# Gated linear attention and an expert layer in one kernel: units of two chunks, position pairs, weights by the quarter

## The chip, the cores and the metric

One core of one Trainium2 chip. The metric is the device time of one execution in microseconds (us). Five engines work side by side: PE (matmul; PEld is its weight load), VectorE (DVE), ScalarE (ACT), GpSimd (POOL) and SyncE (SP, here a queue of DMA issues). The kernel fixes the order of instructions on each engine itself.

## The reference, cut to what matters

```
f = sigmoid(f_logit)                                  # q, k, v, f_logit: (4, 8, 768, 48), float32
for t in range(768):                                  # for each of 4 batches and 8 heads
    state = f[t, :, None] * state + outer(k[t], v[t]) # 48 x 48
    y[t] = q[t] @ state
x = y, heads side by side                             # (3072, 384)
h = x @ w_in                                          # (3072, 2048)
out = (0.5 * h * (1 + erf(h / sqrt(2)))) @ w_out      # (3072, 384), float32
```

## The kernel before

The 768 positions of each batch are cut into six chunks of 128, 24 chunks in all, with a position on each partition and the eight heads side by side. A chunk is loaded by four DMAs of SP, f_logit, k, q and v (L299 and L302), each 192 KB in runs of 48 floats, 192 bytes. ScalarE makes exp and ln of f_logit (L319, L323); PE sums the logs down the chunk with a triangular matrix (L335) and makes the chunk's total decay (L337); ScalarE takes exp of both signs (rg L341, gt L344, gl L347); VectorE multiplies k and q by them (L350, L354); GpSimd casts v (L358). In `attn(n)` PE turns k and q so that the head dimension lies on partitions (L378), VectorE copies them out (kq, L383), PE makes the scores of four pairs of heads in eight matmuls (L392), VectorE masks them (L396). PE makes the chunk's own state (L406), VectorE and GpSimd carry the state from chunk to chunk (L417, L421, L423, L428), PE adds the carried state's part and the chunk's own part of y (L442, L448). VectorE copies y out (L454), PE turns it (L462), VectorE writes it as the columns of x that belong to the chunk (L464).

The second half works on groups of chunks (`SIZES`: four groups of one, then ten of two). F1 multiplies x by `w_in` in blocks that fill one PSUM bank (L485), ScalarE puts each block through gelu (L490), F2 multiplies by `w_out` (L500), ScalarE copies the result out (L504) and SP stores it (L506). Both weights are bf16 tiles in SBUF, one for each matrix (`win`, `wout`, L201 and L202), each loaded in four quarters by GpSimd's DMA queue, which also casts them from float32 (L305, L309).

The order comes from a planner (`Plan.run`, L90): each operation has an engine, an estimated duration, what it reads and writes, and buffers; the operation with the earliest possible start is placed next, a tie is broken by `prio`. An ACT operation that needs the other table (exp and ln in one, gelu in the other) has its start put 2 x 1.28 us later for the comparison. The planner's order is then issued as it stands, engine by engine. `LOADS` fixes the order of the loads: chunks 0 to 3, the four quarters of `win` (i0 to i3), chunk 4, two quarters of `wout` (o0, o1), chunk 5, o2, o3, then the rest. Where the next load is on another queue than the one before it, it waits for the landing of an earlier load on that other queue: the third before it for a load of GpSimd, the second before it for a load of SP. SP also issues the stores, in the planner's order.

PSUM has eight banks: four for F1 and F2 (`s_fh`), two for the scores (`s_ap`), two for all else (`s_m`).

Of the kernel before, what the change touches and what calls it, by code (L numbers as in the profile page):

```python
# [16 lines left out]
TABLE = 1.28  # L17

# [37 lines left out]
class Op:  # L56
    __slots__ = ("eng", "dur", "fn", "bufs", "prio", "deps", "table", "start", "end", "vis", "seq", "name",
                 "left", "outs", "inst", "gate")


class Plan:
# [6 lines left out]
    def add(self, eng, dur, fn, rd=(), wr=(), bufs=(), prio=0.0, deps=(), table=None, name=""):  # L68
# [3 lines left out]
        o.gate = ()  # L72
        o.seq = len(self.ops)
        d = list(deps)
# [15 lines left out]
    def run(self):  # L90
        free = dict.fromkeys(list(LAT), 0.0)
# [9 lines left out]
        while ready:  # L101
            best = None
            for o in ready:
                t = free[o.eng]
                for d in o.deps:
                    v = d.end if d.eng == o.eng and o.eng != "DMA" else d.vis
                    t = v if v > t else t
# [12 lines left out]
                if o.table and act and o.table != act:  # L120
                    x += 2 * TABLE
# [40 lines left out]
def kernel(  # L162
# [36 lines left out]
    mask = one.tile([C, C], BF16, name="mask")  # L199
    negcol = one.tile([C, 1], BF16, name="negcol")  # L200
# [10 lines left out]
    s_gl = slots(10, [C, P2], F32, "gl")  # L211
    s_kq = slots(3, [C, 2, P2, C], BF16, "kq")
    s_am = slots(6, [C, P2, C], BF16, "am")
# [15 lines left out]
    P.add("POOL", 0.5, lambda: tri(trin, -1.0), wr=["trin"], prio=-100)  # L229
    P.add("POOL", 0.5, lambda: make_identity(nc, ident), wr=["ident"], prio=-90)  # L230
    P.add("POOL", 0.5, lambda: tri(mask, 1.0), wr=["mask"], prio=-80)
    P.add("POOL", 0.1, lambda: nc.gpsimd.memset(negcol, -1.0), wr=["negcol"], prio=-99)
# [19 lines left out]
    n = 0  # L252
    els = []
    for s in ELS:
        els.append(dict(ns=list(range(n, n + s)), fl=s_fl.new(), lf=s_lf.new()))
        for j in range(s):
            X[n + j].update(el=els[-1], j=j)
        n += s
    for n in range(NCH):
        for nm in ("kt", "qt", "vt"):  # L260
            X[n][nm] = s_in[nm].new()
# [3 lines left out]
    order = []  # L265

    def load(eng, what, issue, wr, bufs, dur, name):
# [5 lines left out]
        def fn():  # L273
            o.inst = issue()
            if i and order[i - 1][0] != eng:
                back = 3 if eng == "pool" else 2
                for j in range(i - back, -1, -1):
                    if order[j][0] != eng and order[j][1].inst is not None:
                        tc.add_manual_dep(
                            o.inst.ins, order[j][1].inst.ins.name,  # L280
                            mybir.DependencyInfo(mybir.DependencyClass.Sync, mybir.DependencyReason.DATA),
                            reason="one transfer after another")
                        break
        o.fn = fn
        return o
# [7 lines left out]
    last = None  # L293
    for what in LOADS:
        m = int(what[1:])
        if what[0] == "c":
            x = X[m]
            e = x["el"]
            load("sp", "f", lambda x=x, e=e, m=m: nc.sync.dma_start(out=e["fl"].t()[:, x["j"]], in_=src(f_logit, m)),  # L299
                 [("f", m)], [e["fl"]], 1.03, f"ldf{m}")  # L300
            for nm, a in (("kt", k), ("qt", q), ("vt", v)):
                load("sp", nm, lambda x=x, nm=nm, a=a, m=m: nc.sync.dma_start(out=x[nm].t(), in_=src(a, m)),  # L302
                     [(nm, m)], [x[nm]], 1.03, f"ld{nm}{m}")
        elif what[0] == "i":
            load("pool", what, lambda m=m: nc.gpsimd.dma_start(  # L305
                out=win[:, :, 512 * m:512 * m + 512], in_=win_src[:, :, 512 * m:512 * m + 512]),
                [f"win{m}"], [], 2.2, what)
        else:
            load("pool", what, lambda m=m: nc.gpsimd.dma_start(out=wout[:, 4 * m:4 * m + 4, :], in_=wo_src[m]),  # L309
                 [f"wout{m}"], [], 2.2, what)  # L310


    def decays(lo, hi, gate):
        made = []
        pr0 = 10 * lo
        for e in [e for e in els if lo <= e["ns"][0] < hi]:
            ns, s, fl, lf = e["ns"], len(e["ns"]), e["fl"], e["lf"]
            pr = 10 * ns[0]
            made.append(P.add("ACT", 0.04 + 0.34 * s, lambda fl=fl, s=s: nc.scalar.activation(  # L319
                fl.t()[:, 0:s], fl.t()[:, 0:s], AF.Exp, scale=-1.0),  # L320
                rd=[("f", n) for n in ns], wr=[("e", n) for n in ns], bufs=[fl], table="exp", prio=pr, deps=gate,
                name=f"E{ns[0]}"))
            P.add("ACT", 0.04 + 0.34 * s, lambda fl=fl, lf=lf, s=s: nc.scalar.activation(  # L323
                lf.t()[:, 0:s, :, 0:D], fl.t()[:, 0:s], AF.Ln, bias=1.0),
                rd=[("e", n) for n in ns] + z_lf, wr=[("lf", n) for n in ns], bufs=[fl, lf], table="exp", prio=pr,
                name=f"L{ns[0]}")
            for j, n in enumerate(ns):
                x = X[n]
# [236 lines left out]
```

## Time and profile before

| | us |
|---|---|
| median of three runs | 228.24 |
| the three runs | 226.05, 228.24, 228.71 |
| the profiled execution | 228.91 |
| its span, first to last instruction | 227.1 |
| PE busy in it | 187.8 (83%) |
| ACT busy | 126.5 (56%) |
| DVE busy | 103.8 (46%) |
| POOL busy | 49.0 (22%) |
| mean granted clock of PE | 0.985 |

Busy times are of one profiled execution. A busy PE is not PE at its peak, since a wait for weights and a lower clock count as busy too. What an engine waited for is inferred from semaphores.

### The profile page before, as it was taken

What the parts mean: (1) busy time and instruction counts of PE and PEld (TensorE: products, weight loads), DVE (VectorE), ACT (ScalarE), POOL (GpSimd) and SP (SyncE); (2) the same over time, 40 slices, a digit from 0 to 9 for tenths busy, and PEclk for the clock granted to TensorE, in tenths of its full rate; (3) what the DMA queues carried; (4) which work ended last, traced back from release to release, by engine and by line L of the source; (5) the groups of instructions that cost most, each with busy time, mean ns of one, the idle gap of its engine ahead of it and who ended that gap; (6) DMA issues with size and microseconds to landing.
All of it is one profiled execution on the core that took longest, in us unless ns stands there. A gap on an engine that the chain in (4) does not pass through costs nothing. (4 is left out here: it accounts for less than half of the span.)

```text
span 227.1 us, 4959 instructions
## 1 busy us (share of the span) xinstructions
PE 187.8 (83%) x1984; PEld 147.7 (65%) x1984; DVE 103.8 (46%) x210; ACT 126.5 (56%) x234; POOL 49.0 (22%) x99
## 2 busy tenths in 40 slices
PE   0666436199896789979969968999999999999993
PEld 0444236199564577767758657778788696878871
DVE  3788401000174374795887849779767200000000
ACT  4444022049622848597588687869297182736550
POOL 2236231302020150342226035233211000000000
PEclk9999999999999589999999999999999999999999
DMA  7998437998708994999999899981020001010101
GB/s 133 187 187 119 71 42 138 160 178 141 143 32 211 190 194 74 196 198 179 207 202 184 168 205 197 184 179 36 0 72 4 35 35 38 35 67 6 69 0 71
DMA packets 105495, 27.06 MB, mean 119 GB/s; under 512 B 100352, under 2 KB 104960, under 8 KB 105472
## 3 DMA queue, kind: packets, MB, share of 16 engines
q1 hardware_dynamic: 103296, 23.60, 55.3%
q0 software_dynamic: 2176, 3.15, 9.1%
q8 instruction: 15, 0.25, 0.5%
q14 instruction: 8, 0.07, 0.1%
HBM read 25.17 MB, written 4.72 MB: 132 GB/s over the span
## 5 line engine op out<-in xcount | busy, mean ns | idle before, releaser
L485 PE MATMUL ps<-xT,win 128*128 128x256 bf16 (+1 forms) x672 | 77.4, 275 | 13.8 <-DMA win<-in_moe_w_in_dram 13.4
L485 PEld LDWEIGHTS <-win 128*128 128x128 bf16 x672 | 67.0, 119 | 16.5 <-DMA win<-in_moe_w_in_dram 14.1
L490 ACT ACTIVATE gT<-ps 128x512 bf16<-128x512 f32 x96 | 55.1, 600 | 37.0 <-PE ps L485 34.0
L500 PE MATMUL ps<-wout,gT 128*128 128x384 bf16 x384 | 68.9, 326 | 0.0
L500 PEld LDWEIGHTS <-gT 128*128 128x128 bf16 x384 | 35.7, 98 | 20.1
L396 DVE TENSOR_TENSOR am<-ps,mask 128x512 bf16<-128x512 f32 x48 | 31.3, 684 | 3.5 <-PE ps L392 3.2
L350 DVE TENSOR_TENSOR kp<-kt,rg 128x384 bf16<-128x384 f32 x24 | 14.4, 602 | 34.3 <-ACT rg L341 34.1
L504 ACT ACTIVATE osb<-ps 128x384 f32<-128x384 f32 x24 | 11.8, 490 | 31.9 <-PE ps L500 31.9
L358 POOL CAST vb<-vt 128x384 bf16<-128x384 f32 x24 | 13.1, 546 | 58.6 <-DMA vt<-in_v_dram 58.5
L454 DVE CAST yb<-ps 128x384 bf16<-128x384 f32 x24 | 13.3, 555 | 22.3 <-PE ps L448 22.1
L423 POOL TENSOR_TENSOR tn<-rr,gl 128x384 f32<-128x384 f32 x16 | 14.1, 883 | 32.1 <-DVE rr L421 23.5
L319 ACT ACTIVATE fl<-fl 128x768 f32<-128x768 f32 (+1 forms) x14 | 10.5, 753 | 16.4 <-DMA fl<-in_f_logit_dram 16.4
L383 DVE COPY kq<-ps 128x1024 bf16<-128x1024 bf16 x24 | 16.3, 685 | 4.9 <-PE ps L378 3.4
L341 ACT ACTIVATE rg<-ps 128x384 f32<-128x384 f32 x24 | 11.9, 496 | 10.7 <-PE ps L337 10.5
L428 POOL CAST sb<-tn 48x192 bf16<-48x192 f32 x40 | 15.0, 374 | 8.6 <-DVE tn L417 6.6
L531 ACT ACT_TABLE_LOAD x13 | 16.7, 1283 | 0.2
L335 PE MATMUL ps<-lf,trin 128*128 128x384 bf16 x24 | 8.7, 369 | 9.8 <-ACT lf L323 7.5
L354 DVE TENSOR_TENSOR qp<-qt,gt 128x384 bf16<-128x384 f32 x24 | 15.4, 640 | 0.0
L337 PEld LDWEIGHTS <-lf 128*128 128x128 bf16 x96 | 6.2, 102 | 11.4 <-issue 10.1
L378 PE MATMUL ps<-ident,kp 128*128 128x128 bf16 x96 | 10.4, 237 | 2.4 <-DVE kp L350 1.2
L392 PE MATMUL ps<-kq 64*128 64x128 bf16 x192 | 10.4, 233 | 2.5 <-DVE kq L383 2.5
L344 ACT ACTIVATE gt<-ps 128x384 f32<-128x384 f32 x24 | 11.9, 495 | 0.0
(37 smaller groups left out, 142.6 us busy)
## 6 DMA issues: line engine op xcount, KB each, us to landing
fl<-in_f_logit_dram SPq DMA_DIRECT2D x24, 192.0 KB, 4.6
kt<-in_k_dram SPq DMA_DIRECT2D x24, 192.0 KB, 4.5
qt<-in_q_dram SPq DMA_DIRECT2D x24, 192.0 KB, 4.5
vt<-in_v_dram SPq DMA_DIRECT2D x24, 192.0 KB, 4.3
out_dram<-osb SPq DMA_DIRECT2D x24, 192.0 KB, 2.0
win<-in_moe_w_in_dram POOLq DMA_DIRECT2D x4, 384.0 KB, 5.0
wout<-in_moe_w_out_dram POOLq DMA_DIRECT2D x4, 384.0 KB, 6.5
```

The costliest lines, as they stand in the source:

```text
L350: P.add("DVE", 0.475, lambda x=x, rg=rg: nc.vector.tensor_tensor(x["kp"].t()[:, :, 0:D], x["kt"].t(), rg.t().rearrange("p (h d) -> p h d", ...
L354: P.add("DVE", 0.475, lambda x=x, gt=gt: nc.vector.tensor_tensor(x["qp"].t()[:, :, 0:D], x["qt"].t(), gt.t().rearrange("p (h d) -> p h d", ...
L358: P.add("POOL", 0.47, lambda x=x: nc.gpsimd.tensor_copy(x["vb"].t(), x["vt"].t().rearrange("p h d -> p (h d)")), rd=[("vt", n)], wr=[("vb" ...
L383: P.add("DVE", 0.61, lambda: nc.vector.tensor_copy(kq.t(), tpv()), rd=[("tk", n), ("tq", n)], wr=[("kq", n)], bufs=[tp, kq], prio=pr + 4, ...
L396: P.add("DVE", 0.61, lambda hh=hh: nc.vector.tensor_tensor(ams[hh].t(), aps[hh].t().rearrange("p (h t) -> p h t", t=C), mask.unsqueeze(1). ...
L423: P.add("POOL", 0.83, lambda: nc.gpsimd.tensor_tensor(tn.t(), rr.t(), glb(), ALU.mult), rd=[("rr", n), ("gl", n)], wr=[("tn", n)], bufs=[r ...
L428: P.add("POOL", 0.36, lambda hh=hh: nc.gpsimd.tensor_copy(sb.t()[64 * hh:64 * hh + D, :, D * hh:D * hh + D], tn.t()[64 * hh:64 * hh + D, : ...
L454: P.add("DVE", 0.475, lambda: nc.vector.tensor_copy(yb.t(), yp.t()[:, 0:HD]), rd=[("yp", n)], wr=[("yb", n)], bufs=[yp, yb], prio=pr + 2, ...
L485: nc.tensor.matmul(hps.t()[:, i * tok:(i + 1) * tok], col(fo)[:, kk, :], xT.t()[:, kk, :], start=(kk == 0), stop=(kk == KO - 1))
L490: acts.append(P.add("ACT", 0.50, lambda u=u, hps=hps: nc.scalar.activation(gT.t()[:, u * pk:(u + 1) * pk, :].rearrange("p a b -> p (a b)") ...
L500: nc.tensor.matmul(op.t()[:, 0:d_model], gT.t()[:, fo, s_ * C:(s_ + 1) * C], wout[:, fo, :], start=(fo == 0), stop=(fo == FO - 1))
L531: nc.scalar.preload_act_table_set({"exp": "natural_log_exp_and_others", "gelu": "gelu_and_others"}[o.table])
```

## The change

The unit of work becomes two chunks for everything: `SIZES` is twelve groups of two, a unit's f_logit, k, q and v lie in one tile each, and a unit has one exp, one ln and, after one kq copy for each chunk, the scores of both. Units 0, 1 and 2 are loaded as position pairs: a partition p holds positions 2p and 2p + 1 of the 256, which lie side by side in memory, so that one DMA loads 384 KB in runs of 384 bytes. The unit's first 64 partitions are then its first chunk and the other 64 its second, and each of the two "halves" of the tile holds the even or the odd positions of both. So the sums use block matrices (`trip`, `negp`), the scores are made in 64x64 tiles with a mask of their own (`maskp`), two for each pair of heads and half, 32 matmuls in a unit; the states of the two chunks are 16 matmuls over 64 partitions, y is 32, and the carried state's part is a step of its own (YX). The copy of x puts the positions back in order. The other nine units are loaded and computed as before, chunk by chunk.

The weights lie in one tile for each quarter. `LOADS` becomes units 0 and 1, `win`, unit 2, `wout`, the rest. The planner now knows the waits between loads and GpSimd's time for an issue (0.8 us), starts its clocks at 0.7 and 1.8 us, and holds a table switch back by at most 2.0 us (`PATIENCE`) from when the operation became ready. The diff, cut to its core:

```diff
+PATIENCE = 2.0
...
-                    x += 2 * TABLE
+                    x = max(t, min(t + 2 * TABLE, max([d.vis for d in o.deps] + [0.0]) + PATIENCE))
...
-SIZES = [1, 1, 1, 1, 2, 2, 2, 2, 2, 2, 2, 2, 2, 2]
-PHASES = ['X0:1', 'G0:1', 'X1:2', 'G1:2', 'X2:3', 'G2:3', 'X3:4', 'G3:4', 'X4:6', 'G4:5', 'X6:8', 'G5:6', 'X8:10', 'G6:7', 'X10:12', 'G7:8', 'X12:14', 'G8:9', 'X14:16', 'G9:10', 'X16:18', 'G10:11', 'X18:20', 'G11:12', 'X20:22', 'G12:13', 'X22:24', 'G13:14']
-ELS = [1, 1, 1, 1, 2, 2, 2, 2, 2, 2, 2, 2, 2, 2]
-LOADS = ['c0', 'c1', 'c2', 'c3', 'i0', 'i1', 'i2', 'i3', 'c4', 'o0', 'o1', 'c5', 'o2', 'o3']
-LOADS += [f"c{n}" for n in range(6, 24)]
+
+SIZES = [2] * 12
+PAIRS = [0, 1, 2]
+LOADS = ["u0", "u1", "i0", "i1", "i2", "i3", "u2", "o0", "o1", "o2", "o3"]
+LOADS += [f"u{n}" for n in range(12) if f"u{n}" not in LOADS]
...
-    win = one.tile([C, KO, d_ff], BF16, name="win")
-    wout = one.tile([C, FO, d_model], BF16, name="wout")
+    win = [one.tile([C, KO, 512], BF16, name=f"win{i}") for i in range(4)]
+    wout = [one.tile([C, 4, d_model], BF16, name=f"wout{i}") for i in range(4)]
...
-    s_in = {n: slots(8, [C, H, D], F32, n) for n in ("kt", "qt", "vt")}
-    s_fl = slots(4, [C, 2, H, D], F32, "fl")
+    NU = NCH // 2
+    s_in = {n: slots(4, [C, 2 * HD], F32, n) for n in ("kt", "qt", "vt")}
+    s_fl = slots(3, [C, 2 * HD], F32, "fl")
...
-    s_kq = slots(3, [C, 2, P2, C], BF16, "kq")
-    s_am = slots(6, [C, P2, C], BF16, "am")
+    s_gl = slots(6, [C, 2, P2], F32, "gl")
+    s_kq = slots(3, [C, 2, P2, 2, C], BF16, "kq")
+    s_am = slots(8, [C, P2, C], BF16, "am")
...
+    def pair_sums():
+        nc.gpsimd.memset(trip, 0.0)
+        nc.gpsimd.memset(negp, 0.0)
+        for c in range(2):
+            r = slice(64 * c, 64 * c + 64)
+            nc.gpsimd.memset(negp[r, c:c + 1], -1.0)
+            for st in range(2):
+                blk = trip[r, st, r]
+                nc.gpsimd.affine_select(out=blk, in_=blk, compare_op=ALU.is_ge if st else ALU.is_gt, fill=-1.0,
+                                        base=0, pattern=[[-1, 64]], channel_multiplier=1)
+
+    def pair_mask():
+        nc.gpsimd.memset(maskp, 0.0)
+        for c in range(2):
+            r = slice(64 * c, 64 * c + 64)
+            for jk in range(2):
+                for jq in range(2):
+                    blk = maskp[r, jk, jq]
+                    nc.gpsimd.affine_select(out=blk, in_=blk, compare_op=ALU.is_ge if jk > jq else ALU.is_gt, fill=1.0,
+                                            base=0, pattern=[[-1, 64]], channel_multiplier=1)
+    P.add("POOL", 1.9, pair_sums, wr=["trip", "negp"], prio=-100)
+    P.add("POOL", 2.6, pair_mask, wr=["maskp"], prio=-85)
...
+    U = [dict(fl=s_fl.new(), lf=s_lf.new(), pair=u in PAIRS, **{nm: s_in[nm].new() for nm in s_in}) for u in range(NU)]
...
+    def load(eng, issue, wr, bufs, dur, name):
         i = len(order)
-        o = P.add("DMA", dur, None, wr=wr, bufs=bufs, prio=i, name=name)
-        o.table = None
+        gate = None
+        if i and order[i - 1][0] != eng:
+            back = 3 if eng == "pool" else 2
+            for j in range(i - back, -1, -1):
+                if order[j][0] != eng:
...
+        prev = order[-1][1] if order else None
+        gd = [gate] if gate is not None else []
+        if eng == "pool":
+            if pools:
+                gd.append(pools[-1])
+            k = P.add("POOL", 0.8, None, deps=gd, prio=-1000 + i, name="i" + name)
+            o = P.add("DMA", dur, lambda: None, wr=wr, bufs=bufs, prio=i, name=name, chain=prev, deps=[k])
+            k.fn = lambda o=o: fn(o)
...
+    def srcp(a, u):
+        b, c = divmod(2 * u, nC)
+        return a[b, :, c * C:(c + 2) * C, :].rearrange("h (p j) d -> p h (j d)", j=2)
...
+            if x["pair"]:
+                for nm, a in names:
+                    load("sp", lambda x=x, nm=nm, a=a, m=m: nc.sync.dma_start(
+                        out=x[nm].t().rearrange("p (h x) -> p h x", h=H), in_=srcp(a, m)),
+                        [(nm, 2 * m), (nm, 2 * m + 1)], [x[nm]], 1.2, f"{nm}{m}")
+            else:
+                for j in range(2):
+                    for nm, a in names:
+                        load("sp", lambda x=x, nm=nm, a=a, m=m, j=j: nc.sync.dma_start(
+                            out=half(m, x[nm], j), in_=src(a, 2 * m + j)),
+                            [(nm, 2 * m + j)], [x[nm]], 1.05, f"{nm}{m}.{j}")
...
+            load("pool", lambda m=m: nc.gpsimd.dma_start(out=win[m], in_=win_src[:, :, 512 * m:512 * m + 512]),
+                 [f"win{m}"], [], 2.2, what)
...
+                nc.tensor.matmul(g[:, 0:HD], trip[:, 0, :], lf.t()[:, 0, :, 0:D], start=True, stop=False)
+                nc.tensor.matmul(g[:, 0:HD], trip[:, 1 - j, :], lf.t()[:, 1, :, 0:D], start=False, stop=True)
+                if j:
+                    for i in range(2):
+                        for p in range(P2):
+                            nc.tensor.matmul(g[:, HD + 2 * p:HD + 2 * p + 2], lf.t()[:, i, 2 * p:2 * p + 2, :], negp,
+                                             start=False, stop=(i == 1), skip_group_check=True)
...
+    def attn_pair(u):
...
+            def amm(jk=jk, aps=aps):
+                for p in range(P2):
+                    for cc in range(2):
+                        for hh in range(2):
+                            r, t = slice(64 * hh, 64 * hh + 64), slice(64 * cc, 64 * cc + 64)
+                            nc.tensor.matmul(aps[hh].t()[t, p * C:(p + 1) * C],
+                                             kq.t()[r, 0, p, cc, 64 * jk:64 * jk + 64], kq.t()[r, 1, p, cc, :],
+                                             start=True, stop=True)
+            P.add("PE", 0.45, amm, rd=[("kq", n) for n in ns], wr=[("ap", u, jk)], bufs=[kq] + aps + ams[-1],
...
+        def smm():
+            for p in range(P2):
+                for jk in range(2):
+                    for cc in range(len(sps)):
+                        r = slice(64 * cc, 64 * cc + 64)
+                        nc.tensor.matmul(sps[cc].t()[:, 96 * p:96 * p + 96], kps[jk].t()[r, 2 * p:2 * p + 2, :],
+                                         vbs[jk].t()[r, 96 * p:96 * p + 96], start=(p == 0 and jk == 0), stop=(jk == 1),
+                                         skip_group_check=True)
...
+        def intra():
+            for hh in range(2):
+                for p in range(P2):
+                    h = 2 * p + hh
+                    for jk in range(2):
+                        for cc in range(2):
+                            r = slice(64 * cc, 64 * cc + 64)
+                            nc.tensor.matmul(yps[cc].t()[:, D * h:D * h + D], ams[jk][hh].t()[r, p, :],
+                                             vbs[jk].t()[r, D * h:D * h + D], start=(h == 0 and jk == 0),
+                                             stop=(cc == 0 and osb is None and hh == 1 and p == P2 - 1 and jk == 1),
+                                             skip_group_check=True)
...
+            P.add("PE", 0.26, lambda cc=cc, o=o: inter(yps[cc], lambda p: kq.t()[:, 1, p, cc, :], o, False),
+                  rd=[("yi", n), ("sb", n - 1, 0), ("sb", n - 1, 1)] + [("kq", m) for m in ns], wr=[("yp", n)],
+                  bufs=[yps[cc], kq, o], prio=pr + 2 + 10 * cc, name=f"YX{n}")
...
-            return win[:, :, 512 * (fo // 4):512 * (fo // 4) + 512].rearrange("p kk (c j) -> p kk j c", j=4)[:, :, fo % 4, :]
+            return win[fo // 4].rearrange("p kk (c j) -> p kk j c", j=4)[:, :, fo % 4, :]
...
+    for u in range(NU):
+        decays(u)
+        (attn_pair if U[u]["pair"] else attn_nat)(u)
+        while g < NG and first[g] + SIZES[g] <= 2 * u + 2:
+            ffn_group(g, ())
+            g += 1
```

## Rows read from the trace of the kernel before

**Rows 1.** Windows: stages of the span, all engines; DMA share of 16 engines.

```profile
core 0: us, PE busy (x) PEld busy (x) DVE busy (x) ACT busy (x) POOL busy (x), PEclk, DMA share, GB/s
...
5.68:17.00 11.32, 7.36 (x78) 5.13 (x79) 9.22 (x17) 5.27 (x15) 3.15 (x6) 1.00 1.45 187
...
20.00:44.75 24.75, 9.80 (x99) 8.18 (x98) 6.43 (x12) 4.47 (x8) 7.77 (x13) 1.00 0.67 104
...
56.80:85.00 28.20, 23.33 (x225) 16.50 (x223) 14.23 (x26) 14.21 (x28) 5.87 (x11) 0.88 0.77 154
85.00:142.00 57.00, 51.05 (x626) 40.06 (x625) 42.29 (x80) 42.49 (x81) 18.42 (x35) 1.00 0.96 181
...
180.00:227.10 47.10, 43.36 (x330) 34.25 (x328) 0.00 (x0) 23.52 (x41) 0.00 (x0) 1.00 0.12 43
```

**Rows 2.** Waits: engine and line, for what; us in total, times, longest.

```profile
PE ps L485 <- DMA win<-in_moe_w_in_dram: 13.4, 3, 5.7
POOL win L305 <- PE ps L485: 12.7, 2, 6.4
```

**Rows 3.** Timeline, 18 to 45 us: start, us, instruction, idle before it and its releaser.

```profile
18.03 0.93 POOL L305 DMA_DIRECT2D win<-in_moe_w_in_dram  x1
...
30.64 0.78 POOL L305 DMA_DIRECT2D win<-in_moe_w_in_dram  x1 [6.41 <-PE ps L485]
...
35.40 0.37 SPq L299 DMA_DIRECT2D fl<-in_f_logit_dram  x1
...
38.96 0.80 POOL L305 DMA_DIRECT2D win<-in_moe_w_in_dram  x1 [6.28 <-PE ps L485]
...
44.76 10.83 PE L485 MATMUL ps<-xT,win 128*128 128x128 bf16 x143 [5.67 <-DMA win<-in_moe_w_in_dram]
```

**Rows 4.** Timeline, the start.

```profile
1.02 0.29 POOL L225 TENSOR_SCALAR_AFFINE_SELECT trin<-trin 128x128 bf16<-128x128 bf16 x1
...
3.79 0.52 ACT L319 ACTIVATE fl<-fl 128x384 f32<-128x384 f32 x1 [1.77 <-DMA fl<-in_f_logit_dram]
...
8.01 0.52 ACT L319 ACTIVATE fl<-fl 128x384 f32<-128x384 f32 x1 [1.55 <-DMA fl<-in_f_logit_dram]
...
12.83 0.35 DVE L464 COPY xT<-ps 128x384 bf16<-128x384 bf16 x1
```

**Rows 5.** The page: the queue of the weight loads, and one such load's landing.

```profile
q0 software_dynamic: 2176, 3.15, 9.1%
...
win<-in_moe_w_in_dram POOLq DMA_DIRECT2D x4, 384.0 KB, 5.0
```

**Rows 6.** The chain that ended last: start, us, what.

```profile
159.12 0.45 PE ps L378 x8
...
161.52 0.17 PE ps L442 x4
161.69 0.20 PE ps L448 x8
161.89 0.33 PE ps L392 x8
...
163.24 0.17 PE ps L462 x3
...
167.20 0.16 PE ps L335
...
168.11 0.17 PE ps L406 x4
...
181.60 5.24 PE ps L485 x48
186.84 5.20 PE ps L500 x32
```

**Rows 7.** Groups by line and form: busy us, mean ns | idle before.

```profile
L531 ACT ACT_TABLE_LOAD x13 | 16.7, 1283 | 0.2
...
L392 PEld LDWEIGHTS <-kq 64*128 64x128 bf16 x192 | 5.9, 100 | 6.5 <-DVE kq L383 3.8 <-issue 1.2 <-DVE yb L454 0.4
```

More of the change, by code (lines that the diff above doesn't have):

```diff
@@ L105, in run @@
                 for d in o.deps:
-                    v = d.end if d.eng == o.eng and o.eng != "DMA" else d.vis
+                    v = d.end if d.eng == o.eng and (o.eng != "DMA" or d is o.chain) else d.vis
                     t = v if v > t else t
@@ L251 @@
     X = [{} for _ in range(NCH)]
[L252 to L267, printed above, removed]
-        i = len(order)
-        o = P.add("DMA", dur, None, wr=wr, bufs=bufs, prio=i, name=name)
-        o.table = None
-        order.append((eng, o))
[L273 to L285, printed above, removed]
@@ new lines, with half, fn @@
+    U = [dict(fl=s_fl.new(), lf=s_lf.new(), pair=u in PAIRS, **{nm: s_in[nm].new() for nm in s_in}) for u in range(NU)]
+    def half(u, b, j):
+        if U[u]["pair"]:
+            return b.t().rearrange("p (h j d) -> p j h d", j=2, d=D)[:, j]
+        return b.t().rearrange("p (j h d) -> p j h d", j=2, d=D)[:, j]
+    order, pools = [], []
+    def load(eng, issue, wr, bufs, dur, name):
+        i = len(order)
+        gate = None
[3 more added lines that the diff above has]
+                if order[j][0] != eng:
+                    gate = order[j][1]
+                    break
+        def fn(o):
+            ins = issue()
+            o.inst = ins
+            if gate is not None:
+                tc.add_manual_dep(
+                    ins.ins, gate.inst.ins.name,
+                    mybir.DependencyInfo(mybir.DependencyClass.Sync, mybir.DependencyReason.DATA),
+                    reason="one transfer after another")
+        prev = order[-1][1] if order else None
[6 more added lines that the diff above has]
+            k.fn = lambda o=o: fn(o)
+            pools.append(k)
+        else:
+            o = P.add("DMA", dur, None, wr=wr, bufs=bufs, prio=i, name=name, chain=prev, deps=gd)
+            o.fn = lambda o=o: fn(o)
+        order.append((eng, o))
@@ new lines, with decays, lnop, cum @@
+            load("pool", lambda m=m: nc.gpsimd.dma_start(out=win[m], in_=win_src[:, :, 512 * m:512 * m + 512]),
+                 [f"win{m}"], [], 2.2, what)
+        else:
+            load("pool", lambda m=m: nc.gpsimd.dma_start(out=wout[m], in_=wo_src[m]), [f"wout{m}"], [], 2.2, what)
+    def decays(u):
+        x = U[u]
+        fl, lf, pair = x["fl"], x["lf"], x["pair"]
+        ns = (2 * u, 2 * u + 1)
+        pr = 20 * u
+        x["gl"] = gl = s_gl.new()
+        flv = fl.t
+        P.add("ACT", 0.72, lambda: nc.scalar.activation(fl.t(), fl.t(), AF.Exp, scale=-1.0),
+              rd=[("fl", n) for n in ns], wr=[("e", u)], bufs=[fl], table="exp", prio=pr, name=f"E{u}")
+        def lnop():
+            v = fl.t().rearrange("p (h j d) -> p j h d" if pair else "p (j h d) -> p j h d", j=2, d=D)
+            nc.scalar.activation(lf.t()[:, :, :, 0:D], v, AF.Ln, bias=1.0)
+        P.add("ACT", 0.72, lnop, rd=[("e", u)] + z_lf, wr=[("lf", u)], bufs=[fl, lf], table="exp", prio=pr, name=f"L{u}")
+        gps = [s_m.new(), s_m.new()]
+        for j, n in enumerate(ns):
+            y = X[n]
+            gt, rg = s_gt.new(), s_rg.new()
+            y.update(qp=s_qp.new(), kp=s_kp.new(), vb=s_vb.new())
+            pr = 20 * u + 10 * j
+            def cum(j=j, g=gps[j]):
+                g = g.t()
+                if not pair:
+                    nc.tensor.matmul(g[:, 0:HD], trin, lf.t()[:, j, :, 0:D], start=True, stop=True)
@@ L395, in attn, with mask_scores @@
+    def mask_scores(aps, ams, key, nm, rd, pr, mk, mkey):
         for hh in range(2):
```

342 lines of the change are left out of this document (183 added, 159 removed).

## The prediction

> **What bounds the kernel now.** I read the windows by stage first, then the waits, then the timeline of the weights, then the chain that ended last. The windows split the span in three kinds of time. From 85 us on PE is nearly full: 51.05 of 57 us, and in the last 47.1 us it has 43.36 us of work while VectorE and GpSimd have nothing left [rows 1]. So the end is set by how much PE work is still to be done when PE becomes continuous. Before that it is not: in 20.00 to 44.75 PE is busy 9.80 of 24.75 us, and the DMA engines, at a share of 0.67 and 104 GB/s, are not full either [rows 1]. Nobody is the bound there; something is waited for. The waits name it: PE waited 13.4 us for `win`, and the GpSimd queue that issues these loads waited 12.7 us for PE at L485, the matmul that reads `win` [rows 2]. The timeline shows the circle: the second-last and the last quarter are issued at 30.64 and 38.96, behind 6.41 and 6.28 us of waiting for L485 matmuls that read the quarters already there, and PE's unbroken run begins at 44.76, after 5.67 us of waiting for the last quarter [rows 3]. All four quarters lie in one tile `win`, read through a strided view, so a write of one is held back by reads of another. The next chunk's load stands behind the third quarter in the chain of transfers and is issued only at 35.40 [rows 3].
>
> **The change, part by part.** The sum is made against the profiled execution: span 227.1, time 228.91, so 1.8 us outside the span; the median is 0.7 below that time.
>
> *One tile per quarter.* It removes the two waits of 6.41 and 6.28 us [rows 2, 3]. What is then last for the quarters is the order of transfers: `i0` waits for `kt` of unit 1, the sixth load.
>
> *Position pairs.* A load of a pair unit is 1024 packets of 384 bytes where two loads of 1024 packets of 192 bytes were. The pace of the old ones: chunk 0 to chunk 1 takes 8.01 - 3.79 = 4.22 us for four loads, 1.05 each [rows 4]. The new price is in no row: it lies between 1.05 (a packet costs the same) and 2.1 (a byte costs the same). In 5.68 to 17.00 the loads move 187 GB/s, 11.7 per engine, 16.4 ns a packet of 192 bytes; in 180.00 to 227.10, where only stores of 1536 bytes a row run, 0.12 x 16 engines x 47.1 us move 43 GB/s x 47.1 us, 69 ns a packet [rows 1]. A straight line between the two gives 24 ns at 384 bytes, times 64 packets an engine: 1.5 us. I take 1.5; both ends stay for the range.
> So the first load, which landed for ACT at 3.79, lands near 4.2, and `kt` of unit 1 at 4.2 + 5 x 1.5 = 11.7. The issue of `i0` costs 0.93 [rows 3] and 5.0 to land [rows 5]: 17.6. The queue of the weights takes 9.1% of 227.1 us for eight loads [rows 5], 2.6 each, so `i3` lands near 25.4; unit 2 (gated on `i2`, at 22.8) near 32; the quarters of `wout` from 34 to 42.
>
> *Units of two chunks: when is the first x there?* Chunk 0 took from 3.79 to 12.83 + 0.35 [rows 4], about 9.5 us from its load. A pair adds to this chain: exp and ln over 768 columns 0.66; rg, gt and the products of the second chunk 1.1; a second kq 0.7; twice the score tiles 0.6; two more masks 1.3; the longer Y 0.8; the second yb, transpose and x copy 1.1. These are estimates from the same chain. Sum 6.3, so x of unit 0 is there at 4.2 + 9.5 + 6.3 = 20.0. `i0` (17.6) is earlier and `i3` (25.4) is not yet needed, as the eight blocks of F1 at PE's lower clock last over 10 us. From 20.0 PE has unbroken work.
>
> *Work in that stretch.* Before it lasted 227.1 - 44.75 = 182.35 us. To it come the F1 of one chunk, which PE had done by then: half of 5.24, 2.6 [rows 6]; the attention of two chunks (four were done by 44.75, now two by 20.0): L378, L442, L448, L392, L462, L335 and L406 make 1.65 a chunk [rows 6], 3.3. The pair units cost PE more matmuls: 16 more score tiles at 0.33/8, eight more state matmuls at 0.17/4, 16 more of Y at 0.20/8 and two more sums at 0.16 [rows 6], together 1.7 a unit, up to 3.4 at the lower clock; units 1 and 2 lie in the stretch: 3.4.
> A row for weights of 64 columns does not exist; the half-height ones of L392 take 100 ns, issued ahead of their matmuls [rows 7]. The Trainium skill (TensorEngine Tiling (Array Packing), Restrictions and Performance sections) says that column tiling switches the fast weight load off and that a change of the tiling mode drains the engine, which speaks against 64x64 tiles. No run here shows it yet; if every one of the 64 score loads of units 1 and 2 cost 100 ns more, the sum would be 6.4 us higher.
>
> *What DMA gives back later.* In 56.8 to 85 PE is idle 28.20 - 23.33 = 4.87 us and the granted clock is 0.88, worth 0.12 x 28.2 = 3.4 us [rows 1]: loads late behind the weights. With the loads some 15 us earlier against PE this goes: -8.25. In 85 to 142 PE is idle 5.95 us with DMA at 0.96 [rows 1]; I take 2 us of it, as DMA is ahead. Is it ahead? Unit 3, gated on `o2` at 39, has its second f near 49 and its x near 62; until then PE has three FFN groups (3 x 10.44 [rows 6]) and two attentions (2 x 5), 41 us plus about 3 at the lower clock, to 64. After that DMA needs 8 x 1.05 = 8.4 us a unit and PE 10.44 + 3.3. So it just holds.
>
> *The planner's patience.* A table switch was held back by 2.56 us against every rival; now by no more than 2.0 us from when the operation became ready. More switches follow. 13 loads of 1.28 us [rows 7]; with one pair a unit it would be some 23, 12.8 us more on ACT. ACT is busy 42.49 of 57 us in 85 to 142 [rows 1], so I let a quarter reach PE: +3.2 (bounds 0 and 12.8). The Trainium skill (ScalarE: Activation LUTs, What ACT_TABLE_LOAD costs) counts 2.66 us a switch with a drain; by that, and the same quarter, it would be 6.7. The trace so far shows 1283 ns a load.
>
> *Put at nothing.* GpSimd builds trip and maskp with five fills and twelve selects of at most 0.29 us [rows 4], under 5 us, the first needed near 6 us; the first loads cover it, without that cover it would be those 5 us. VectorE's permuted copies (six of kq, six of x): none in the trace; at worst twice as long, 1.4 us on unit 0's chain, elsewhere beside PE. GpSimd's issues now stand as planned operations; what is queued behind a gated issue there is the cast of v and the carry of the state, which PE's Y waits for: a gate that comes 2 us late makes x late by as much.
>
> Sum: 20.0 + 182.35 + 2.6 + 3.3 + 3.4 - 8.25 - 2.0 + 3.2 = 204.6; with 1.8 outside and 0.7 to the median, **206 us**.
>
> **The rivals.**
> *A, as above:* 206.
> *B, PE packs tightly:* the rest of the idle time of 85 to 142 (4 us) goes too and table loads hide: 206 - 4 - 3.2 = 199. For it: 24.75 us at a DMA share of 0.67 show how much was waiting for order, not work. Against: L335 and its like still wait on ACT.
> *C, 384-byte packets cost per byte:* 2.1 a load, +0.6 for x of unit 0, but +3.6 on `i0` and +6 on `wout`, so F2 of group 0 starts at 40 where PE runs dry near 38, and unit 3 comes 6 us later than PE needs it: about +6, 212. For it: nothing below 192 or between 192 and 1536 bytes in the rows.
> *D, the order of transfers takes the place of the false wait:* a late gate holds GpSimd's or SP's queue and the weights are complete only at 44.75 as before. PE loses 24.7 us but does the attention of units 1 and 2 meanwhile (2 x 5): 220. For it: SP's issue at 35.40 was such a gate [rows 3]; against: six more microseconds of it came from L485.
> *E, slower: ACT's tables.* With a patience of 2 us gelu and exp take turns within a group. If each load beyond 23 stops PE for its whole 1.28 us, then 232.8 (2% slower) takes (232.8 - 206)/1.28 = 21 more, 44 loads; the place is F1, whose four banks are full after 2.6 us. From some 44 loads on it decides: 233 and more. For it: the key is bounded now and F1 delivers a block every 0.65 us; against: F2's 5.2 us a group [rows 6] leave room for the exps.
>
> **How the numbers follow.** A 0.55, B 0.16, C 0.10, D 0.08, E 0.11. B to C span 199 to 212; with x of unit 0 between 18 and 24 and the bounds of the tables' share (-3.2, +9.6) the range is 196 to 218, and holds A, B and C, 0.81. About 2% can be told from no change here: below 223.7 is faster. Faster: A, B, C and 0.03 of D, 0.84; within 2%: the rest of D, and E with fewer loads, 0.09; slower: 0.07.
>
> **What would show it.** In the profile after: no GpSimd wait for L485 at the `win` loads; the last `win` quarter landed by 26 and PE unbroken from about 20; a f load of a pair every 6 us in the start; 20 to 26 table loads; DMA done by about 115 instead of 153; the end again four groups of FFN alone. Wrong it would be by a PE gap in 30 to 65 (weights or unit 3 late), by over 40 table loads, or by score matmuls well over 0.33 us for eight.

## The result, and the profile after

The changed kernel takes 203.26 us (median of four runs, 202.79 to 203.86) against 227.21 for the kernel before beside it: a ratio of 0.8944, 95% interval 0.8872 to 0.9016. The span of the profiled execution is 200.9 us instead of 227.1. The forecast was 206 in a range of 196 to 218. Some executions of one kernel are over 1.5% slower than its fastest; the ratios leave these out, while the medians below include them.

The windows by stage, as in [rows 1] (us of the stretch, then busy us of each engine, granted clock, DMA share, GB/s):

```profile
0.00:19.60 19.60, 10.66 (x139) 7.69 (x139) 12.97 (x41) 8.20 (x15) 13.19 (x41) 1.00 1.06 203
19.60:33.00 13.40, 11.96 (x153) 9.51 (x154) 7.50 (x14) 5.93 (x9) 5.97 (x12) 1.00 1.09 212
33.00:45.00 12.00, 11.71 (x115) 8.28 (x114) 4.53 (x9) 11.09 (x19) 2.71 (x6) 1.00 0.97 201
45.00:60.00 15.00, 14.23 (x184) 10.78 (x182) 8.51 (x16) 14.12 (x22) 2.56 (x6) 1.00 0.96 200
60.00:85.00 25.00, 23.54 (x282) 18.62 (x282) 17.54 (x34) 23.45 (x40) 8.63 (x17) 1.00 0.95 194
85.00:120.00 35.00, 33.22 (x388) 25.71 (x386) 22.78 (x44) 32.02 (x53) 11.21 (x22) 1.00 0.96 198
120.00:155.00 35.00, 34.62 (x423) 27.48 (x423) 26.99 (x50) 24.85 (x50) 8.12 (x15) 1.00 0.11 35
155.00:200.90 45.90, 42.29 (x341) 33.62 (x340) 2.93 (x6) 23.75 (x41) 0.00 (x0) 1.00 0.11 39
```

PE is nearly full from 19.6 on (11.96 of 13.40 us) where it was full from 44.75; the stage 20.00 to 44.75 of [rows 1], with 9.80 busy of 24.75 us, has no successor. DMA works at 194 to 212 GB/s until 120. ScalarE is now the second tightest engine: 32.02 of 35 us in 85 to 120.

The start and the weights in the timeline, as in [rows 3] and [rows 4]:

```profile
4.59 0.84 ACT L368 ACTIVATE fl<-fl 128x768 f32<-128x768 f32 x1 [2.58 <-DMA fl<-in_f_logit_dram]
...
10.62 0.84 ACT L368 ACTIVATE fl<-fl 128x768 f32<-128x768 f32 x1 [1.65 <-DMA fl<-in_f_logit_dram]
...
12.39 3.26 POOL L355 DMA_DIRECT2D win<-in_moe_w_in_dram  x4 [1.89 <-DMA kt<-in_k_dram]
...
21.09 0.58 DVE L512 COPY xT<-ps 128x384 bf16<-128x384 bf16 x1
...
22.56 2.75 PE L652 MATMUL ps<-xT,win 128*128 128x256 bf16 x12
22.85 0.37 SPq L345 DMA_DIRECT2D fl<-in_f_logit_dram  x1
...
27.02 0.85 ACT L368 ACTIVATE fl<-fl 128x768 f32<-128x768 f32 x1 [10.53 <-DMA fl<-in_f_logit_dram]
27.89 1.28 ACT L692 ACT_TABLE_LOAD   x1
...
28.78 2.21 POOL L358 DMA_DIRECT2D wout<-in_moe_w_out_dram  x4 [3.35 <-DMA kt<-in_k_dram]
...
29.18 3.04 ACT L657 ACTIVATE gT<-ps 128x512 bf16<-128x512 f32 x6
...
38.94 1.47 PE L652 MATMUL ps<-xT,win 128*128 128x256 bf16 x12
...
48.19 0.84 ACT L368 ACTIVATE fl<-fl 128x768 f32<-128x768 f32 x1
```

All four quarters of `win` go out in one piece from 12.39, behind a landed `kt` and no matmul. x of unit 0 is complete at 21.67 and F1 begins at 22.56, at about half of PE's later rate (12 matmuls in 2.75 us, at 38.94 in 1.47), although the granted-clock column reads 1.00 there. ScalarE stands idle for 10.53 us before unit 2's exp.

Groups by line and form, as in [rows 7] (busy us, mean ns | idle before):

```profile
L692 ACT ACT_TABLE_LOAD x29 | 37.2, 1283 | 0.5
...
L583 PEld LDWEIGHTS <-kq 64*64 64x64 bf16 x96 | 2.6, 137 | 3.1 <-issue 2.6 <-DVE kq L449 0.3
...
L617 PEld LDWEIGHTS <-am 64*128 64x128 bf16 x96 | 1.7, 99 | 0.6 <-issue 0.5
```

Table loads have gone from 13 to 29, that is from 16.7 to 37.2 us of ScalarE. The next section shows what the rule that adds them is worth.

### The profile page after: what moved, and what is told of

Its sections match the earlier page's. It is cut to its first block, busy times and chain, and to the rows that moved or that the text cites. A ratio compares the mean times of both kernels' runs of the same rounds, so it can differ in the third digit from the quotient of the medians.

```text
span 200.9 us, 4982 instructions
## 1 busy us (share of the span) xinstructions
PE 182.2 (91%) x2010; PEld 141.7 (71%) x2010; DVE 103.7 (52%) x210; ACT 143.4 (71%) x243; POOL 52.4 (26%) x116
## 4 chain that ended last, share of the span: by engine, by line
PE 57%; ACT 20%; DMA 13%; SPq 3%; issue 3%; DVE 2%; POOL 1%; ACTq 0%; DVEq 0%
PE ps L667 25%; PE ps L652 20%; ACT L692 8%; ACT gT L657 6%; DMA fl<-in_f_logit_dram 5%; DMA win<-in_moe_w_in_dram 4%; DMA kt<-in_k_dram 3%; PE ps L444 3%; SPq L345 2%; ACT fl L368 2%; PE ps L535 2%; ACT lf L373 2%; PE ps L506 1%; ACT rg L400 1%; PE ps L385 1%
## 5 line engine op out<-in xcount | busy, mean ns | idle before, releaser
L652 PE MATMUL ps<-xT,win 128*128 128x256 bf16 x576 | 72.7, 277 | 3.1 <-ACT gT L657 3.0
L667 PE MATMUL ps<-wout,gT 128*128 128x384 bf16 x384 | 70.1, 326 | 0.4 <-DMA wout<-in_moe_w_out_dram 0.2
L652 PEld LDWEIGHTS <-win 128*128 128x128 bf16 x576 | 61.4, 115 | 6.0 <-issue 3.5
L657 ACT ACTIVATE gT<-ps 128x512 bf16<-128x512 f32 x96 | 53.1, 602 | 7.9 <-PE ps L652 5.6
L692 ACT ACT_TABLE_LOAD x29 | 37.2, 1283 | 0.5
L456 DVE TENSOR_TENSOR am<-ps,mask 128x512 bf16<-128x512 f32 x36 | 23.1, 684 | 5.9 <-PE ps L535 5.8
L368 ACT ACTIVATE fl<-fl 128x768 f32<-128x768 f32 x12 | 10.3, 859 | 18.0 <-DMA fl<-in_f_logit_dram 17.9
L449 DVE COPY kq<-ps 128x1024 bf16<-128x1024 bf16 x24 | 16.4, 685 | 3.3 <-PE ps L444 3.1
L416 DVE TENSOR_TENSOR qp<-qt,gt 128x384 bf16<-128x384 f32 x24 | 14.4, 601 | 0.2 <-ACT gt L402 0.2
L456 DVE TENSOR_TENSOR am<-ps,maskp 128x512 bf16<-128x512 f32 x12 | 7.7, 685 | 5.4 <-PE ps L583 5.4
L444 PE MATMUL ps<-ident,qp 128*128 128x128 bf16 x96 | 10.2, 234 | 0.3 <-DVE qp L416 0.3
L373 ACT ACTIVATE lf<-fl 128x768 bf16<-128x768 f32 x12 | 10.1, 843 | 0.3
```

The costliest lines, as they stand in the source:

```text
L368: P.add("ACT", 0.72, lambda: nc.scalar.activation(fl.t(), fl.t(), AF.Exp, scale=-1.0), rd=[("fl", n) for n in ns], wr=[("e", u)], bufs=[fl ...
L373: nc.scalar.activation(lf.t()[:, :, :, 0:D], v, AF.Ln, bias=1.0)
L416: P.add("DVE", 0.475, lambda y=y, gt=gt, j=j: nc.vector.tensor_tensor(y["qp"].t()[:, :, 0:D], half(u, x["qt"], j), gt.t().rearrange("p (h ...
L444: nc.tensor.transpose(tpv()[:, i, p, :], sr.t()[:, 2 * p:2 * p + 2, :], ident)
L449: P.add("DVE", 0.61, lambda tpv=tpv, kqv=kqv: nc.vector.tensor_copy(kqv(), tpv().rearrange("a i p (c t) -> a (i p) c t", c=2) if U[u]["pai ...
L456: P.add("DVE", 0.61, lambda hh=hh: nc.vector.tensor_tensor(ams[hh].t(), aps[hh].t().rearrange("p (h t) -> p h t", t=C), mk.unsqueeze(1).to ...
```

## The experiments

Each kernel was timed beside the kernel before, whose median was 226.15 to 226.64 in these runs. Sizes in us are differences of medians unless the ratio is named; taken from the ratios, some differ by up to 2.5 us. Two theories stood at first: that the false wait of the quarters is most of the gain, or that the order and size of the loads set the start.

**Split alone.** The kernel before with nothing but this:

```diff
-    win = one.tile([C, KO, d_ff], BF16, name="win")
-    wout = one.tile([C, FO, d_model], BF16, name="wout")
+    win = [one.tile([C, KO, 512], BF16, name=f"win{i}") for i in range(4)]
+    wout = [one.tile([C, 4, d_model], BF16, name=f"wout{i}") for i in range(4)]
```

> The kernel before, with nothing changed but one tile for each quarter of both weights; same loads, same planned order. Theory 1 (the false wait of the quarters is most of the gain): GpSimd's 12.7 us of waiting for L485 are gone, the last win quarter is there near 32 instead of 44.7, chunk 4's load goes out near 30 instead of 35.4, and the time falls by 9 to 12 us, to 215 to 218. Theory 2 (the loads' order and size set the start, the false wait was only one of several waits that end close together): under 5 us, to 222 to 226.

Measured 217.8 us, ratio 0.9602 (0.9527 to 0.9677). The GpSimd rows of [rows 3] become:

```profile
18.11 0.93 POOL L305 DMA_DIRECT2D win<-in_moe_w_in_dram  x1
...
22.95 0.81 POOL L305 DMA_DIRECT2D win<-in_moe_w_in_dram  x1
...
24.25 0.78 POOL L305 DMA_DIRECT2D win<-in_moe_w_in_dram  x1
...
27.59 0.80 POOL L305 DMA_DIRECT2D win<-in_moe_w_in_dram  x1
```

The third quarter goes out at 24.25 instead of 30.64, the last at 27.59 instead of 38.96, with no wait for L485. The false wait is real, and worth about 8.4 us by itself (9 by the ratio), a third of the gain and not most of it.

**One tile.** The changed kernel with the two lines the other way round, its order untouched.

> The changed kernel with both weights back in one tile each; same order. Theory 1 taken plainly (the split itself brings the gain) expects 10 us or more back: 213 and over. Theory 2 (in the changed order all four quarters are issued by 16 us, before any matmul reads win, so there is nothing left to hold back) expects only that the first block of F1 waits for the last quarter, from about 22.6 to 25: 204 to 206.

Measured 204.37, ratio 0.9030 (0.8975 to 0.9084), which overlaps the changed kernel's interval. Its PE timeline has the one trace that the single tile leaves:

```profile
22.40 0.40 PE L652 MATMUL ps<-xT,win 128*128 128x256 bf16 x1
24.23 2.51 PE L652 MATMUL ps<-xT,win 128*128 128x256 bf16 x11 [1.43 <-DMA win<-in_moe_w_in_dram]
```

One matmul runs, then 1.43 us pass until the last quarter has landed. So the same edit is worth 8.4 us in the old order and 1 to 2, not told apart from none, in the new one, where the loads go out before anything reads the tile.

**No pairs.** `PAIRS = []`, nothing else.

> The changed kernel with no position pairs: all twelve units are loaded chunk by chunk, 192-byte runs, natural scores. By the prediction's prices 16 loads at 1.05 replace 8 at 1.5 ahead of win: kt of unit 1 lands near 18 instead of 12, all quarters 6 us later, f of unit 0 complete at 8 instead of 4.6, and PE saves 1.7 us a unit of extra matmuls. Theory 1: 4 to 6 us slower than the changed kernel, 207 to 209. Rival (DMA is hidden anyway once the false wait is gone): within 1 us of 203.3. Rival (a pair's extra matmuls eat the saving): 201 to 203.

Measured 204.96, ratio 0.9054 (0.8988 to 0.9119), overlapping again. The pairs are worth some 2 us (1.7 by the medians, 2.5 by the ratio), not told apart from none, and not the 4 to 6 of the theory. F1 begins at 22.24 in its trace, no later than with pairs. Its rows for the first exp and the last x copy of unit 0:

```profile
7.29 0.84 ACT L368 ACTIVATE fl<-fl 128x768 f32<-128x768 f32 x1 [5.28 <-DMA fl<-in_f_logit_dram]
...
20.97 0.34 DVE L514 COPY xT<-ps 128x384 bf16<-128x384 bf16 x1
```

The exp needs f of both chunks and comes 2.7 us later than with pairs, but the chain from there to x is 3.1 us shorter (14.0 us against 17.1): what pairs save before the first exp they lose again on the way to x. `win` is issued from 16.11 and `wout` from 34.21, 4 and 5 us later, and PE idles 2.3 us in 33 to 45 and 2.5 us in 45 to 60.

**Patience off.** The changed kernel with the old price of a table switch:

```diff
-PATIENCE = 2.0
+PATIENCE = 1000.0
```

> The changed kernel with the old price of a table switch (2.56 us against every rival, no limit): 11 table loads instead of 29 in its order, so 23 us less on ACT. If the loads cost PE a quarter of their time, as the prediction has it for the ten it counted, it is some 5 us faster: 198. If the switches earn their price (the next unit's exps come earlier and PE's attention fills the F1 gaps), it is slower: 206 to 210. If they are hidden: within 1 us of 203.3.

Measured 220.54, ratio 0.9750 (0.9689 to 0.9811): 17.3 us of the 24 are gone with one constant. 18 loads fewer (11 instead of 29), and slower. Its windows and its ScalarE timeline show how:

```profile
45.00:60.00 15.00, 15.00 (x123) 12.81 (x121) 0.00 (x0) 9.33 (x17) 1.06 (x3) 1.00 0.98 206
60.00:85.00 25.00, 17.63 (x162) 12.64 (x161) 13.19 (x25) 14.98 (x30) 7.27 (x14) 0.72 0.91 187
```

```profile
46.19 5.18 ACT L657 ACTIVATE gT<-ps 128x512 bf16<-128x512 f32 x8 [0.16 <-PE ps L652]
...
56.63 5.18 ACT L657 ACTIVATE gT<-ps 128x512 bf16<-128x512 f32 x8 [0.16 <-PE ps L652]
...
66.97 1.28 ACT L692 ACT_TABLE_LOAD   x1
68.26 0.84 ACT L368 ACTIVATE fl<-fl 128x768 f32<-128x768 f32 x1
```

From 46 to 67 ScalarE does two groups of gelu with no switch between. The last load of unit 3's f is issued at 43.51, and its exp comes at 68.26, with no wait for DMA; in the changed kernel it comes at 48.19. Meanwhile VectorE has nothing at all to do for 15 us, no new x is made, and when the stock of FFN work is used up PE is busy 17.63 of 25 us, at a granted clock of 0.72. In the changed kernel the same stretch is 23.54 of 25 at 1.00.

Another value of the constant gives another order of the whole kernel, so the 17.3 us belong to that order; the late exps are what its trace shows of it.

So a third theory: a late exp starves PE a group later, and table loads are cheap against that. The next four runs asked whether patience and split together are the change, and where the price of the loads begins.

**Patience in the kernel before**, and **with split tiles there**:

```diff
-                    x += 2 * TABLE
+                    x = max(t, min(t + 2 * TABLE, max([d.vis for d in o.deps] + [0.0]) + PATIENCE))
```

> The kernel before with only the planner's rule for a table switch changed (held back no longer than 2.0 us from when the operation became ready): 27 table loads instead of 13. New theory after the last four runs (a late exp starves PE of attention, and the switches are cheap against that): in the kernel before the stretch 56.8 to 85 loses 8 us by idle time and the lower clock, of which a part is late exps: 218 to 223. Rival (patience is worth something only once the loads come early; before, exps wait for DMA): 225 to 229, or slower by the 14 extra loads at a quarter, 4.5 us: 231.

> The kernel before with the split tiles and the new rule for a table switch, nothing else (chunks, loads and the planner's picture of the loads as before). Theory (split 8.4 us and patience 17 us are the change; pairs and units are small): 200 to 206. Rival (the planner must know the waits between the loads, or the rule acts on wrong times): 212 to 218.

Measured 225.5, ratio 0.9947 (0.9870 to 1.0023), and 216.73, ratio 0.9600 (0.9529 to 0.9670), the ratio of the split alone. The rule that carries 17 us in the changed kernel is worth nothing in the old one, with 27 loads in both. ScalarE's row for the first two-chunk exp of the kernel with split and patience suggests why:

```profile
46.04 0.84 ACT L320 ACTIVATE fl<-fl 128x768 f32<-128x768 f32 x1 [4.76 <-DMA fl<-in_f_logit_dram]
```

There the exp waits for its data, not for its turn, and later ones that do not wait for DMA come no earlier by the rule: at 78.38 and 98.36, against 78.76 and 97.71 with the split alone. The third theory in its plain form falls; by these rows patience pays only where the old price had made an exp late.

**Half a microsecond, and four.** `PATIENCE = 0.5` and `PATIENCE = 4.0` in the changed kernel.

> The changed kernel with a patience of 0.5 us instead of 2.0: 37 table loads instead of 29, 10 us more on ACT. Theory (early exps matter, a load is cheap): within 2 us of 203.3. Rival (ACT is near its bound, 32.0 of 35 us busy in 85 to 120): each further load costs PE its 1.28 us: 210 and more.

> The changed kernel with a patience of 4.0 us: 21 table loads, with the old price's cap of 2.56 us still there, so only operations ready for over 1.44 us gain. Theory: exps are still let in within 4 us, so most of the 17 us stays: 203 to 207. If the loads themselves cost anything, it is faster than 203.3 by up to 2 us.

Measured 210.78, ratio 0.9232 (0.9148 to 0.9317), and 205.62, ratio 0.9080 (0.9013 to 0.9148). Eight loads more than 29 cost 6.5 us by the ratios, 0.8 each; eight fewer cost some 2 to 3 us at most likely, but the interval still touches that of the changed kernel (up to 0.9016). With 0.5 us gelu and exp take turns over one unit:

```profile
33.00:45.00 12.00, 11.44 (x96) 8.90 (x97) 1.72 (x3) 11.88 (x18) 0.48 (x2) 1.00 0.91 184
45.00:60.00 15.00, 12.79 (x173) 8.72 (x171) 10.81 (x20) 10.21 (x22) 6.54 (x12) 0.91 1.01 213
```

In the first of these stretches ScalarE is busy 11.88 of 12 us and VectorE 1.72: the exp of unit 2 starts at 30.13 and its last decay is ready only at 48.4 (27.02 and 40.3 in the changed kernel). PE pays in the second: 12.79 of 15 us, where the changed kernel has 14.23. Too many switches delay the decays just as too few do.

**What is left.** Between 216.73 and 203.26 stand the planner's picture of the loads, the order, the units and the pairs. The changed kernel with the old picture, and the old kernel with split, patience and the new picture, then also with chunks 4 and 5 ahead of `wout`:

```diff
-            k = P.add("POOL", 0.8, None, deps=gd, prio=-1000 + i, name="i" + name)
-            o = P.add("DMA", dur, lambda: None, wr=wr, bufs=bufs, prio=i, name=name, chain=prev, deps=[k])
+        o = P.add("DMA", dur, None, wr=wr, bufs=bufs, prio=i, name=name)
```

```diff
-LOADS = [..., 'c4', 'o0', 'o1', 'c5', 'o2', 'o3']
+LOADS = [..., 'c4', 'c5', 'o0', 'o1', 'o2', 'o3']
```

> The changed kernel (units, pairs, split weights, order of loads, patience 2.0) with the planner's old picture of the loads: it does not know the waits between transfers nor GpSimd's time for an issue, and its clocks start at zero; the chip still waits as before. Theory P (the remaining 13.5 us between the old kernel with split and patience, 216.7, and 203.3 come from the planner seeing when loads really land): 212 to 218, with exps or casts queued ahead of work that is ready. Rival U (units of two, and the order of loads bring it): 203 to 207.

> The old chunks, groups and order of loads with split weights, patience 2.0 and the planner's new picture of the loads. Theory P: 203 to 208. Rival U: 213 to 217, within 3 us of the 216.7 without that picture.

> As the kernel beside it, with chunks 4 and 5 both ahead of all of wout, as in the changed order of loads, which leaves two changes of queue instead of four. If the alternation (each change of queue waits for a landing) costs what the idle DMA of the stretch suggests, 3 to 6 us faster than it; if the old units are what costs, within 1.5 us of it.

Measured 207.79, ratio 0.9253 (0.9137 to 0.9370); 212.79, ratio 0.9468 (0.9344 to 0.9592); and 210.57, ratio 0.9373 (0.9275 to 0.9470). Neither theory has it alone: the picture is worth 4.5 us in the changed kernel (7 by the ratios), where the intervals lie apart, and some 4 in the old one, where they overlap; the order is worth some 2, not told apart from none. The last step, from 210.57 to the kernel without pairs at 204.96, is units of two with all that hangs on them (groups of two from the start, one exp and one ln a unit, the scores after both kq copies, and other buffer counts and estimated durations): 5.6 us, with intervals that lie apart (0.9275 to 0.9470 against 0.8988 to 0.9119). No run takes it apart, but the windows from 40 to 60 show where part of it lies, first with the old units, then with the new ones and no pairs:

```profile
40.00:60.00 20.00, 17.62 (x147) 11.62 (x147) 8.13 (x15) 4.79 (x11) 2.31 (x5) 0.83 0.76 156
40.00:60.00 20.00, 16.95 (x174) 12.17 (x174) 10.83 (x21) 11.47 (x24) 3.44 (x6) 1.00 0.82 176
```

With the old units PE waits 3.71 us for the ln of chunks 4 and 5, until 41.63, and the granted clock of the stretch reads 0.83 instead of 1.00; 0.17 of 17.62 busy us are 3.0 us.

In the changed kernel with the old picture GpSimd's queue reads:

```profile
12.13 0.94 POOL L340 DMA_DIRECT2D win<-in_moe_w_in_dram  x1 [1.92 <-DMA kt<-in_k_dram]
14.75 0.50 POOL L404 CAST vb<-vt 128x384 bf16<-128x384 f32 x1 [1.69 <-DMA vt<-in_v_dram]
...
17.61 0.81 POOL L340 DMA_DIRECT2D win<-in_moe_w_in_dram  x1
...
19.92 1.55 POOL L340 DMA_DIRECT2D win<-in_moe_w_in_dram  x2
```

Casts and carries of the state stand between the issues; the last quarters go out at 19.92 instead of by 15.65, unit 2's f, gated on the third quarter, at 25.05 instead of 22.85, its exp runs at 30.07 instead of 27.02, the first gelus wait behind it, and PE waits 3.77 us for them before its matmuls at 32.87.

**Unit 2 early.** A try for more: unit 2 between the second and third quarter of `win`, so that ScalarE does not stand idle for 10.53 us.

```diff
-LOADS = ["u0", "u1", "i0", "i1", "i2", "i3", "u2", ...
+LOADS = ["u0", "u1", "i0", "i1", "u2", "i2", "i3", ...
```

> The changed kernel with unit 2 loaded between the second and the third quarter of win. In the changed kernel ScalarE sits idle from 16.5 to 27.0 for unit 2's f while F1 blocks wait for gelu from 24 on. With unit 2 some 5 us earlier its exp runs before gelu begins and the exp no longer splits the first gelus. Expected: 200 to 202 if that wait is on the path; 203 to 205 if the later third and fourth quarters and the two more changes of queue take it back.

Measured 202.17, ratio 0.8994 (0.8890 to 0.9097): not to be told apart from 0.8944. ScalarE's rows:

```profile
21.62 0.84 ACT L368 ACTIVATE fl<-fl 128x768 f32<-128x768 f32 x1 [5.72 <-DMA fl<-in_f_logit_dram]
...
26.71 0.49 ACT L402 ACTIVATE gt<-ps 128x384 f32<-128x384 f32 x1
27.21 1.28 ACT L692 ACT_TABLE_LOAD   x1
28.51 2.56 ACT L657 ACTIVATE gT<-ps 128x512 bf16<-128x512 f32 x5
```

The exp comes 5.4 us earlier, as intended, but the planner then puts rg and gt of unit 2's first half ahead of the gelus too, and those begin at 28.51 instead of 29.18. The idle time was moved, not used.

## Why the prediction was right, and where it was not

The total was right, and the mechanism of the start as well. One term of the sum had the wrong sign, and another would not have been there without it, so the nearness of 206 to 203.26 is partly luck.

*The bound and the false wait: right.* PE starts its unbroken run some 22 us earlier. But the prediction ascribed the lost stage to the wait on `win` without saying that the new order all but undoes it by itself: there the split is worth 1 to 2 us (one tile), not 8.4.

*The price of 384 bytes: right.* (10.62 - 4.59)/4 = 1.51 us a load, 1.5 was said. `i0` goes out at 12.39 (11.7 said), unit 2's f at 22.85 (22.8 said); the first quarter of `wout`, issued at 28.78, lets F2 start at 33.60 (34 said for its landing). Rival C is out. What the price bought was not asked there: the pairs are worth some 2 us, not told apart from none.

*x of unit 0: 20.0 said, 21.67 measured.* The chain is 17.1 us from the first exp to the last x copy, where 9.5 + 6.3 were said from the load. VectorE takes unit 1's products in between, 12.97 busy of 19.60 us. Of the permuted copies, those of kq cost nothing more (685 ns), those of x 588 ns instead of 348, inside the bound that the prediction set.

*The extra matmuls of a pair: mis-sized.* 1.7 us a unit were counted at the natural price of 41 ns a score matmul. The PE rows of unit 2, and of a natural unit after it:

```profile
43.74 0.42 PE L583 MATMUL ps<-kq 64*64 64x128 bf16 x16
44.09 2.16 PE L652 MATMUL ps<-xT,win 128*128 128x256 bf16 x18
...
48.60 0.57 PE L617 MATMUL ps<-vb,am 64*128 64x48 bf16 x32
...
58.68 0.40 PE L535 MATMUL ps<-kq 64*128 64x128 bf16 x8 [0.69 <-DVE kq L449]
...
61.89 0.36 PE L557 MATMUL ps<-vb,am 128*128 128x48 bf16 x8
```

Sixteen 64x64 tiles take what eight 64x128 tiles take, and 32 matmuls of Y take 0.57 us where two chunks' 16 take 0.72: a pair's scores and Y, 1.06 of the 1.7 us, cost about nothing more. What is left of the 3.4, the further sums and state matmuls as they were counted, is 1.3. The Trainium skill's rule that column tiling loses the fast weight load (TensorEngine Tiling (Array Packing), Restrictions) has little to show for it here: in unit 2 a load of 64x64 takes 106 ns where one of 64x128 takes 94 (58 to 66 us), not the 100 ns more that the prediction feared. The 137 ns of the group's row include units 0 and 1, which ran at half of PE's rate (153 and 160 ns). Sixteen such loads lie within 0.26 us beside each other. The drain at a change of the tiling mode, which stands in the Trainium skill (TensorEngine Tiling (Array Packing)) under Key Properties, leaves no visible gap either: the scores of unit 2 end at 44.16, and the full-size F1 matmuls start at 44.09.

*What DMA gives back: said 10.25, measured 8.2.* Before, idle time and the lower clock from 44.75 on made 14.3 us (4.87, 3.4 and 5.95 from [rows 1], 0.1 in the rest); after, PE's idle time from 19.6 to 155 sums to 6.1 us, and the clock column reads 1.00. The lower rate of the first F1 blocks, which the column does not show, is left out of both: before, 19 of the 143 matmuls from 44.76 start in the first 2 us and 38 in 2 us from 50.76 on.

*The planner's patience: the step that failed.* The prediction priced the loads that the rule adds (+3.2) and not what the rule is for. With the rule taken out the kernel is 17.3 us slower and the stretch 60 to 85 is at 17.63 of 25 us and a clock of 0.72, worse than the 56.8 to 85 of [rows 1] (23.33 of 28.20 at 0.88). The give-back of the step above was therefore never a matter of DMA alone: f landed early, but without the rule its exp waits some 20 us for its turn. It was there to be read in the code: the price of 2.56 us against every rival holds an exp back for as long as gelus keep coming every 0.65 us. The Trainium skill's figure of 2.66 us a switch (ScalarE: Activation LUTs, What ACT_TABLE_LOAD costs) is not borne out: from the end of unit 2's exp at 27.87 to the gelu at 29.18, with a switch between, are 1.31 us. Nor is a switch's time simply lost on the path: eight loads fewer, at a patience of 4 us, made the kernel no faster, and the eight more at half a microsecond cost 0.8 us each, delay of the decays included.

*Not priced: the planner's picture of the loads and units of two.* They stood in the prediction as work moved or put at nothing; the runs give them some 4.5 and 5.6 us. The errors offset in part: a cost of 3.2 that was not there and 2.1 of the 3.4 for extra matmuls, against a give-back that was 2 us smaller and an x that was 1.7 us later. That makes 1.6 of the 2.7 us between 206 and 203.26; the rest is not accounted for.

*The rivals.* D did not come: no gate holds the weights to 44. E did not come either, with 29 loads, but the harm from switches begins lower than it said: not at 44 loads, since 37 already cost 6.5 us. It is not E's mechanism that the trace shows there: while the loads take turns with gelu PE is busy 11.44 of 12 us, not stopped at F1, and it loses its time after that, for want of attention work. Of what was to be seen: the end is four FFN groups alone (yes), table loads 20 to 26 (29), DMA done by 115 (120).

## What to carry to other kernels

When two kinds of work share an engine with a price for switching, price the switch against what the waiting work feeds, not only in its own time: too few switches starved PE a group later (17.3 us), too many did the same by delay (6.5 us), and the best of the four values tried lay between, with its upper neighbour not clearly worse. A change of several parts is to be priced in combination: the split was worth 8.4 us in the old order and 1 to 2 in the new, and the rule for switches nothing in the old and 17 in the new, as each removes a wait only if it is the one that ends last. An order planned ahead is only as good as its picture of the transfers: a planner that knows when loads land gained 4 to 4.5 us with no other work changed (clear of noise in the changed kernel only).

## What the runs showed of the hardware that was not expected

A packet of 384 bytes costs 1.51 us x 16 / 1024 = 23.6 ns an engine, where one of 192 bytes costs 16.4: neither a price a packet nor a price a byte. Sixteen 64x64 tiles with 128 columns moving take 0.42 us, as long as eight 64x128 tiles (0.40), though each of their weight loads is a little longer at the same rate (106 ns against 94). And the clock column can miss the lower level at the start: in 19.60 to 33.00 it reads 1.00 for the changed kernel, whose first 12 F1 matmuls take 2.75 us; the kernel with unit 2 early has the same 2.75 us for the same 12, from 22.21, and its column reads 0.50 from 20 to 25:

```profile
20.00:25.00 5.00, 4.51 (x54) 2.99 (x56) 2.94 (x5) 1.69 (x2) 1.52 (x2) 0.50 1.13 265
```

The kernel before, too, reads 1.00 while its F1 matmuls from 44.76 run at half the pace of those from 50.76. There the duration of a known matmul is the better witness.
